# Stores and raw weight loads issued by GpSimd, and the reload of operands issued inside a group's last unit

## The chip, the cores and the metric

The kernel runs on one core of a Trainium2 chip. The metric is the device time of one execution in microseconds, as a median of several runs. A profiled execution has its own time, and its trace has a span, which is the time from the first to the last instruction.

## What is computed

An attention over channels feeds two multilayer perceptrons, for 6016 tokens, 256 channels and a hidden width of 2048:

```python
qn = q / (norm(q, axis=1) + 1e-06);  kn = k / (norm(k, axis=1) + 1e-06)
s = kn.transpose(0, 2, 1) @ qn / tau            # 256 x 256
a = exp(s - max); a /= a.sum(-1) + 1e-09
x = v @ a                                        # 6016 x 256
h = x @ w_in;   x = (h * sigmoid(1.702 * h)) @ w_out        # first perceptron
h = x @ w_in2;  out = where(h > 0, h, exp(min(h, 0)) - 1) @ w_out2   # second
```

## The kernel before

A first stage (to about 71 us) sums the squares of q and k and their product, makes the softmax, and folds it into the first weight matrix. After it there are two passes, A for the first perceptron and B for the second. The tokens are cut into six **groups** (b = 0 to 5) of 1024 tokens, the last of 896. A group is worked off in eight **units** (p = 0 to 7), each for 256 of the 2048 hidden columns. Pass A runs all its 48 units, then pass B its 48.

In a unit the first matrix product is made by seven products (`product`, i = 1 to 7, called in the order 1, 5, 6, 2, 7, 3, 4) of 2x2 blocks, whose operands are sums and differences of the blocks. Each operand and weight is held as a high and a low part, so a product is three matmuls (L637). Between them stand the 24 matmuls of the second matrix product of the unit before (L730 in pass A), so that a unit of pass A is 45 matmuls. ScalarE evaluates the activation (L667, L668) and copies two products between banks (L878 opens a unit, L885); VectorE adds (L889, L899) and makes low parts (L700).

The seven operands of a group (tiles `xA`, `xB`, one buffer for each i) are in SBUF while its eight units run. They are made well ahead, in the background of earlier units: `operands(kind, b)` casts each high part on ScalarE (L399), subtracts the low part on VectorE (L403) into a staging tile (`xt`; the tag "st" has four buffers and is shared with `w3t`), and stores it to DRAM (`xdA`, `xdB`; L405). `load_x` (L131) brings it back when the group's turn comes. The seven loads of a group are issued behind its predecessor's last unit; load i can only start when the last unit's product i has been made, since there is one buffer.

Pass A's background also prepares the second perceptron's weights: `fetch` loads raw 64-bit weights (L172 for w1 and w3, L177 for w2 and w4; three buffers `raw`, filled again as they are freed), `rounds` turns them into 32-bit floats, `combine_w3` makes the seven sums of w3 and stores them (`w3d`, L301), and `split_lo` stores w4 (`w4d`, L248, from one buffer `w4t`). One round of this work, called far, is put into the background queue in each odd unit of groups 1 to 5. A background generator is advanced eight times in a unit, first in, first out.

Each engine runs its instructions in program order (a manual schedule). All DMAs are issued by SyncE (SP). A DMA that waits for a semaphore holds back all DMAs behind it on that queue.

The lines that put far work and reloads into a unit:

```python
if b and p % 2:
    queue.append(some(1, far))
step(t)
if p == NP - 1:
    finish(*nxt[:2])
    for i in (1, 5, 6, 2, 7, 3, 4):
        load_x(nxt[0], nxt[1], XOP[i])
```

Of the kernel before, what the change touches and what calls it, by code (L numbers as in the profile page):

```python
# [9 lines left out]
F32 = mybir.dt.float32  # L10
# [12 lines left out]
def kernel(  # L23
# [40 lines left out]
    nc = tc.nc  # L64
# [6 lines left out]
    NP = KF // 2  # L71
# [29 lines left out]
    xd = {  # L101
        (kind, b): dr.tile([P, 7, 2, wid[b]], F32, name=f"xd{kind}{b}")
        for kind in "AB"
        for b in range(NG)
    }
    w3d = [dr.tile([P, 2, 2, 7, P], F32, name=f"w3d{i}") for i in range(NP // 2)]
    w4d = [dr.tile([P, 2, 2, C], F32, name=f"w4d{i}") for i in range(NP)]
# [3 lines left out]
    XOP = {1: 0, 2: 1, 3: 2, 4: 3, 5: 4, 6: 5, 7: 6}  # L111
# [13 lines left out]
    def x_tile(kind, b, i):  # L125
        x_t[kind, b, i] = xp.tile([P, 2, BANK], F32R, tag=f"x{i}", name=f"x{kind}")
        return x_t[kind, b, i]

    def load_x(kind, b, i):
        n = wid[b]  # L130
        nc.sync.dma_start(out=x_tile(kind, b, i)[:, :, :n].bitcast(F32), in_=xd[kind, b][:, i, :, :])  # L131
# [13 lines left out]
    order = [("w1", 0), ("w1", 1), ("w2", 0), ("w1", 2), ("w1", 3), ("w2", 1), ("w2", 2)]  # L145
    order += [("w1", 4), ("w1", 5), ("w2", 3), ("w2", 4), ("w1", 6), ("w1", 7)]
    order += [("w2", i) for i in range(5, NWP)]
    NEAR = len(order)
# [7 lines left out]
    w1s = {}  # L156
    state = {"done": -1, "auto": False, "freed": 0}

    def fetch(x=None):

        n = place[x] if x else next(ring, None)
        if n is None:
            return
        name, i = order[n]
        if x:
            t = wts.tile([P, WP, 2], I32, tag=f"wB{ASIDE[x]}", name="raw")
        else:
            t = cv.tile([P, WP, 2], I32, tag="raw", name="raw", bufs=RAWS)
        w = dram[name]
        if name in ("w1", "w3"):  # L170
            f, c = divmod(i, KC)
            nc.sync.dma_start(  # L172
                out=t.rearrange("p f t -> p (f t)"),
                in_=w[c * P:(c + 1) * P, f * WP:(f + 1) * WP].bitcast(I32),
            )
        else:
            nc.sync.dma_start(  # L177
                out=t.rearrange("p (f d) t -> p f (d t)", f=2),
                in_=w[i * 2 * P:(i + 1) * 2 * P, :].bitcast(I32).rearrange(
                    "(f p) d -> p f d", p=P  # L180
                ),
            )
        raws[n] = t
# [32 lines left out]
    ends = {}  # L216
# [16 lines left out]
    def shaped(n):  # L233
        t = live[n].bitcast(F32)
        return t if order[n][0] == "w1" else t.rearrange("p (f d) -> p f d", f=2)
# [6 lines left out]
    def split_lo(n):  # L242
        if order[n][0] == "w3":
            return
        hi, lo = target(n)
        nc.vector.tensor_sub(lo, shaped(n), hi.bitcast(F32))
        if order[n][0] == "w4":
            nc.sync.dma_start(out=w4d[order[n][1]], in_=ends.pop(n).bitcast(F32))  # L248

    def combine(f0, f1, part, done=None):  # L250

# [35 lines left out]
    def combine_w3(n):  # L287

        c = order[n][1] // KC
        ts = {}  # L290

        def part(x, i, m):
            g, i0, k = (0, 0, 3) if i < 3 else (1, 3, 4)
            if (x, g) not in ts:
                ts[x, g] = stage([P, 2, k, P], "w3t")
            return ts[x, g][:, :, i - i0:i - i0 + m, :]

        def store(g):
            r = slice(0, 3) if g == 0 else slice(3, 7)
            for x in range(2):  # L300
                nc.sync.dma_start(out=w3d[c][:, x, :, r, :], in_=ts[x, g].bitcast(F32))  # L301

        return combine(live[n - 1].bitcast(F32), live[n].bitcast(F32), part, store)

# [56 lines left out]
    made = set()  # L361
# [18 lines left out]
    def operands(kind, b, direct=False):  # L380

        n = wid[b]
        t = full.pop((kind, b))
        b11, b12 = (t[:, 0, i * n:(i + 1) * n] for i in range(2))
        b21, b22 = (t[:, 1, i * n:(i + 1) * n] for i in range(2))
        temp = {}

        def sub(i, x, y):
            temp[i] = stg.tile([P, BANK], F32, tag="t", name="tt", bufs=3)
            nc.vector.tensor_sub(temp[i][:, :n], x, y)  # L390

        def tgt(i):
            if direct:
                return x_tile(kind, b, i)
            return stage([P, 2, BANK], "xt")

        def hi(i, x):
            d = hold_t[i] = tgt(i)
            nc.scalar.copy(d[:, 0, :n], x)  # L399

        def lo(i, x):
            d = hold_t[i]
            nc.vector.tensor_sub(d[:, 1, :n], x, d[:, 0, :n].bitcast(F32))  # L403
            if not direct:
                nc.sync.dma_start(out=xd[kind, b][:, i, :, :], in_=d[:, :, :n].bitcast(F32))  # L405

        hold_t = {}
        hi(0, b11)
        sub(4, b12, b11)
        yield False  # L410
        hi(1, b21)
        lo(0, b11)
        yield False
        hi(2, b22)
        lo(1, b21)
        yield False
        hi(4, temp[4][:, :n])
        sub(5, b22, temp[4][:, :n])
        yield False
        lo(2, b22)  # L420
        lo(4, temp[4][:, :n])
        yield False
        hi(5, temp[5][:, :n])
        sub(6, b22, b12)
        yield False
        hi(6, temp[6][:, :n])
        lo(5, temp[5][:, :n])
        yield False
        sub(3, b21, temp[5][:, :n])
        lo(6, temp[6][:, :n])  # L430
        yield False
        hi(3, temp[3][:, :n])
        yield False
        lo(3, temp[3][:, :n])
        made.add((kind, b))
        yield False
# [40 lines left out]
    with tc.manual_schedule():  # L477
        make_identity(nc, ident)

        with ExitStack() as st:  # L480
# [24 lines left out]
            for i, m in enumerate(CHUNKS):  # L505
# [7 lines left out]
                if i == 4:  # L513
                    nc.sync.dma_start(
                        out=tau_sb,
                        in_=tau.rearrange("(o a) -> o a", o=1).to_broadcast([P, 1]),
# [20 lines left out]
                for s in range(m):  # L537
                    for c in range(KC):
# [4 lines left out]
                            start=(j0 + s == 0),  # L543
# [12 lines left out]
            for i in range(2):  # L556
                for c in range(KC):
                    x = i * KC + c
                    nc.tensor.matmul(
                        n_ps[:, x:x + 1], acc[:, i, c * P:(c + 1) * P], ones[:, 0:1],  # L560
                        start=True, stop=True,
# [12 lines left out]
            for c in range(KC):  # L574
                nc.tensor.matmul(
                    rq_ps[:, c * P:(c + 1) * P], rn[:, c:c + 1].to_broadcast([P, P]), ident,
                    start=True, stop=True,
# [13 lines left out]
            for c in range(KC):  # L591
                nc.vector.scalar_tensor_tensor(
                    out=e[:, c, :], in0=s_ps[c][:, :C], scalar=rk[:, c:c + 1], in1=rq,
# [34 lines left out]
        units = [(kind, b, p) for kind in "AB" for b in range(NG) for p in range(NP)]  # L628
        g_t = {}

        def product(dst, i, u, start):
            kind, b, p = u
            n = wid[b]
            w = w_first[kind, p // 2]
            x = x_t[kind, b, XOP[i]]
            for k, (wi, xi) in enumerate(((0, 0), (0, 1), (1, 0))):
                nc.tensor.matmul(  # L637
                    dst[:, :n],
                    w[:, wi, p % 2, WOP[i], :],
                    x[:, xi, :n],  # L640
                    start=(start and k == 0),
                    stop=(k == 2),
                    skip_group_check=True,
                )
# [334 lines left out]
        for b in range(NG):  # L979
# [6 lines left out]
            nxt = units[units.index(("A", b, 7)) + 2]  # L986
            plan_at(nxt, lambda b=b: queue.append(operands("B", b)))

        for t in range(len(units) + 1):
            u = units[t] if t < len(units) else None  # L990
            if u:
                kind, b, p = u
                if kind == "A" and b == 0 and p:
                    need("w2", min(p, NP - 1))
                if u == ("B", 0, 0):
                    passA.close()
                    tp = ctx.enter_context(tc.tile_pool(name="tpB", bufs=1))
                for f in plan.get(u, []):
                    f()
                if kind == "A":  # L1000
                    if b == 0:
                        queue.append(some(12, near) if p < 5 else some(12, last_near))
                    if b and p % 2:
                        queue.append(some(1, far))
            step(t)
            if u is None:
                break

            if p == NP - 1:
                nxt = units[t + 1] if t + 1 < len(units) else None  # L1010
                if nxt:
                    finish(*nxt[:2])
                    for i in (1, 5, 6, 2, 7, 3, 4):
                        load_x(nxt[0], nxt[1], XOP[i])
            if kind == "A" and b == NG - 1:
                if p % 2:
                    c = p // 2
                    nc.sync.dma_start(out=first_weights("B", c).bitcast(F32), in_=w3d[c])
                if p:
                    need("w4", p - 1)  # L1020
                    nc.sync.dma_start(out=second_weights("B", p - 1).bitcast(F32), in_=w4d[p - 1])
                if p == NP - 1:
                    need("w4", p)
            if u == ("B", 0, 0):
                nc.sync.dma_start(out=second_weights("B", NP - 1).bitcast(F32), in_=w4d[NP - 1])
# [29 lines left out]
```

## Time and profile before

| | |
|---|---|
| median of 3 runs | 1117.41 us (1115.81 to 1118.59) |
| profiled execution | 1117.26 us, of which the trace spans 1115.5 us |
| TensorE (PE) busy | 1071.8 us, 96% |
| VectorE (DVE) busy | 818.3 us, 73% |
| ScalarE (ACT) busy | 779.8 us, 70% |
| GpSimd (POOL) busy | 1.9 us, 9 instructions |
| DMA queue of SP | 143.41 MB, 35.3% of 16 engines' span |

PEld is the weight load of TensorE, SPq the DMA-issuing queue of SyncE. In rows, "L637" is line 637 of the kernel, `b<-xA,wAA` says that tiles xA and wAA are read and a PSUM bank b is written, and the bracket at the end says how long the engine had been idle and what ended it. Matmuls are pipelined, so neighbouring PE rows overlap a little.

### The profile page before, as it was taken

The numbers are of one execution on the slowest core, as the hardware profiler recorded it, in microseconds if no ns is written. First come the engines' busy times: TensorE is split into PE (matmuls) and PEld (weight loads), VectorE is DVE, ScalarE is ACT, GpSimd is POOL, SyncE is SP. The second block draws the span as 40 slices with busy tenths as digits, with TensorE's granted clock in tenths as the row PEclk, the third lists the DMA queues.
The fourth block names the chain that finished last, engine by engine and source line by source line (L and its number), as shares of the span: only waits on it lengthen the run. The fifth ranks groups of instructions, "written<-read, shape, count | busy, mean of one in ns | idle before, by whom it ended". The sixth has DMA issues, their size and how long they took to land.

```text
span 1115.5 us, 15490 instructions
## 1 busy us (share of the span) xinstructions
PE 1071.8 (96%) x5846; PEld 934.4 (84%) x5846; DVE 818.3 (73%) x1326; ACT 779.8 (70%) x1463; POOL 1.9 (0%) x9
## 2 busy tenths in 40 slices
PE   7979999998997998998999999999999999999998
PEld 6767878886886887887889899999899999899998
DVE  5888776564664773664634998888888888888886
ACT  5778777765775774875745867867767767777776
POOL 0000000000000000000000000000000000000000
PEclk9999999998998999999999999999999999999999
DMA  9912165236546564543558114003003103003100
GB/s 334 343 49 95 38 240 193 95 126 230 212 169 217 187 256 170 189 151 136 214 197 316 58 66 149 39 1 133 38 1 132 39 1 132 39 1 108 46 1 34
DMA packets 47355, 144.40 MB, mean 129 GB/s; under 512 B 4528, under 2 KB 14000, under 8 KB 46768
## 3 DMA queue, kind: packets, MB, share of 16 engines
q1 hardware_dynamic: 47280, 143.41, 35.3%
q8 instruction: 46, 0.75, 0.3%
q14 instruction: 29, 0.24, 0.1%
HBM read 86.25 MB, written 57.15 MB: 129 GB/s over the span
## 4 chain that ended last, share of the span: by engine, by line
PE 80%; DVE 7%; ACT 6%; DMA 5%; issue 1%; SPq 0%; ACTq 0%; DVEq 0%
PE b L637 36%; PE b L754 20%; PE b L730 20%; DMA qk<-in_k_dram 2%; DMA xA<-xdA 2%; DVE ee L684 1%; DVE gg L689 1%; DMA w4d<-w4t 1%; DVE g L700 1%; PE b L539 1%; ACT ee L673 1%; PE b L448 1%; ACT th L674 1%; PE b L370 1%; ACT g L696 1%
## 5 line engine op out<-in xcount | busy, mean ns | idle before, releaser
L754 PEld LDWEIGHTS b<-wBB,g 128*128 128x128 f32 x2256 | 301.6, 190 | 21.2 <-DVE g L700 2.3
L754 PE MATMUL b<-wBB,g 128*128 128x256 f32 x2256 | 308.9, 282 | 1.3 <-DVE g L700 1.0
L730 PE MATMUL b<-g,wBA 128*128 128x512 f32 (+1 forms) x1152 | 301.3, 390 | 1.7 <-DVE g L700 1.7
L637 PE MATMUL b<-xA,wAA 128*128 128x512 f32 (+1 forms) x1008 | 271.1, 393 | 25.4 <-DMA xA<-xdA 17.7
L637 PE MATMUL b<-xB,wAB 128*128 128x512 f32 (+1 forms) x1008 | 267.8, 389 | 0.2 <-DVE b L889 0.2
L730 PEld LDWEIGHTS b<-g,wBA 128*128 128x128 f32 x1152 | 218.6, 191 | 43.7 <-DVE g L700 2.2
L637 PEld LDWEIGHTS b<-xA,wAA 128*128 128x128 f32 x1008 | 189.8, 190 | 64.8 <-issue 19.3
L637 PEld LDWEIGHTS b<-xB,wAB 128*128 128x128 f32 x1008 | 174.1, 189 | 21.0 <-DVE b L889 0.4
L696 ACT CAST g<-gg 128x512 fp32r<-128x512 f32 (+1 forms) x192 | 118.4, 617 | 93.2 <-DVE gg L689 93.1
L889 DVE TENSOR_TENSOR b<-b,s 128x512 f32<-128x512 f32 (+1 forms) x96 | 66.0, 687 | 145.6 <-PE b L637 142.3
L684 DVE SCALAR_TENSOR_TENSOR ee<-ee,th 128x512 f32<-128x512 f32 (+1 forms) x192 | 129.8, 676 | 31.9 <-ACT th L674 31.7
L667 ACT ACTIVATE g<-b 128x512 fp32r<-128x512 f32 (+1 forms) x144 | 85.0, 591 | 84.2 <-PE b L637 83.8
L700 DVE TENSOR_TENSOR g<-gf,g 128x512 fp32r<-128x512 f32 (+1 forms) x192 | 128.6, 673 | 19.0 <-ACT gf L668 18.7
L700 DVE TENSOR_TENSOR g<-gg,g 128x512 fp32r<-128x512 f32 (+1 forms) x192 | 129.3, 674 | 11.0 <-ACT g L696 6.5
L673 ACT ACTIVATE ee<-b 128x512 f32<-128x512 f32 (+1 forms) x144 | 84.6, 587 | 34.7 <-PE b L637 34.5
L689 DVE SCALAR_TENSOR_TENSOR gg<-b,ee 128x512 f32<-128x512 f32 (+1 forms) x144 | 97.9, 680 | 4.9
L899 DVE TENSOR_TENSOR c<-b,s 128x512 f32<-128x512 f32 (+1 forms) x96 | 64.6, 673 | 41.6 <-PE b L637 41.4
L668 ACT ACTIVATE gf<-b 128x512 f32<-128x512 f32 (+1 forms) x144 | 84.5, 587 | 2.0 <-DVE g L700 1.6
L674 ACT ACTIVATE th<-b 128x512 f32<-128x512 f32 (+1 forms) x144 | 84.1, 584 | 0.0
L878 ACT COPY b<-b 128x512 f32<-128x512 f32 (+1 forms) x96 | 56.3, 587 | 34.3 <-PE b L637 34.2
L885 ACT COPY s<-b 128x512 f32<-128x512 f32 (+1 forms) x96 | 56.2, 586 | 32.4 <-PE b L637 31.9
L539 PE MATMUL b<-qk 128*128 128x256 f32 x188 | 44.5, 394 | 7.4 <-DMA qk<-in_k_dram 7.3
(91 smaller groups left out, 692.3 us busy)
## 6 DMA issues: line engine op xcount, KB each, us to landing
xdB<-xt SPq DMA_DIRECT2D x35, 512.0 KB, 2.9
xB<-xdB SPq DMA_DIRECT2D x35, 512.0 KB, 5.3
xdA<-xt SPq DMA_DIRECT2D x28, 512.0 KB, 2.9
xA<-xdA SPq DMA_DIRECT2D x28, 512.0 KB, 6.4
raw<-in_moe_w_in_dram SPq DMA_DIRECT2D x16, 512.0 KB, 6.1
raw<-in_moe_w_out_dram SPq DMA_DIRECT2D x16, 512.0 KB, 4.0
wAB<-w3d SPq DMA_DIRECT2D x4, 1792.0 KB, 8.5
v_raw<-in_v_dram SPq DMA_DIRECT2D x11, 512.0 KB, 4.5
```

Of the source, the lines that this page charges most:

```text
L637: nc.tensor.matmul(dst[:, :n], w[:, wi, p % 2, WOP[i], :], x[:, xi, :n], start=(start and k == 0), stop=(k == 2), skip_group_check=True,)
L667: nc.scalar.activation(self.sl(ik)[0], h, AF.Gelu_apprx_sigmoid)
L668: nc.scalar.activation(t[:, :n], h, AF.Gelu_apprx_sigmoid)
L673: nc.scalar.activation(e[:, :n], h, AF.Exp)
L674: nc.scalar.activation(t[:, :n], h, AF.Tanh, scale=0.5)
L684: nc.vector.scalar_tensor_tensor(out=e[:, :n], in0=e[:, :n], scalar=1.0, in1=t[:, :n], op0=ALU.add, op1=ALU.mult,)
L689: nc.vector.scalar_tensor_tensor(out=g[:, :n], in0=h, scalar=0.0, in1=e[:, :n], op0=ALU.max, op1=ALU.min)
L696: nc.scalar.copy(self.sl(ik)[0], self.tmp[ik][:, :self.n])
L700: nc.vector.tensor_sub(lo, self.tmp.pop(ik)[:, :self.n], hi.bitcast(F32))
L730: nc.tensor.matmul(bank[a][:, :n], w[:, f, wi, d * P:(d + 1) * P], g[:, gi, k * n:(k + 1) * n], start=fresh((kind, b, a)), stop=(p == NP - ...
L754: nc.tensor.matmul(bank[a][:, s % 2 * C:(s % 2 + 1) * C], g[:, gi, s * P:(s + 1) * P], w[:, f, wi, :], start=fresh((kind, b, a)), stop=(p ...
L889: nc.vector.tensor_add(bank[c][:, :n], bank[b][:, :n], s5[:, :n])
```

## The change

GpSimd now issues the stores of operands (`xdA`, `xdB`), of w3's sums and of w4, and the loads of raw weights of w3 and w4 (those from place NEAR on). SP keeps all other DMAs. The reload of operand i is issued behind product i of a group's last unit, if the next group's operands have been made. Far work is put into the queue in even units instead of odd ones.

```diff
+    def queue_of(n):
+        return nc.gpsimd if n >= NEAR else nc.sync
@@ fetch
-            nc.sync.dma_start(
+            queue_of(n).dma_start(
...
-            nc.sync.dma_start(
+            queue_of(n).dma_start(
@@ split_lo
-            nc.sync.dma_start(out=w4d[order[n][1]], in_=ends.pop(n).bitcast(F32))
+            nc.gpsimd.dma_start(out=w4d[order[n][1]], in_=ends.pop(n).bitcast(F32))
@@ combine_w3
-                nc.sync.dma_start(out=w3d[c][:, x, :, r, :], in_=ts[x, g].bitcast(F32))
+                nc.gpsimd.dma_start(out=w3d[c][:, x, :, r, :], in_=ts[x, g].bitcast(F32))
@@ operands
-                nc.sync.dma_start(out=xd[kind, b][:, i, :, :], in_=d[:, :, :n].bitcast(F32))
+                nc.gpsimd.dma_start(out=xd[kind, b][:, i, :, :], in_=d[:, :, :n].bitcast(F32))
@@
+        loaded = set()
+
+        def load_next(u, i):
+
+            if u[2] < NP - 1 or u not in units[:-1]:
+                return
+            nxt = units[units.index(u) + 1][:2]
+            if nxt in made and nxt + (i,) not in loaded:
+                loaded.add(nxt + (i,))
+                load_x(*nxt, XOP[i])
+
         def product(dst, i, u, start):
+            product_(dst, i, u, start)
+            load_next(u, i)
+
+        def product_(dst, i, u, start):
@@ the loop over units
-                    if b and p % 2:
+                    if b and p % 2 == 0:
                         queue.append(some(1, far))
...
-                        load_x(nxt[0], nxt[1], XOP[i])
+                        load_next(u, i)
```

On SP, ahead of the reload for group 2 of pass A (`xA<-xdA_86`), there stood before (`x7` is a run of seven):

```order
L131 DMA xA<-xdA_85 128x1024 x7
L405 DMA xdB_90<-xt 128x1024 x6
L358 DMA v_raw<-in_v_dram 128x1024
L405 DMA xdB_90<-xt 128x1024
L358 DMA v_raw<-in_v_dram 128x1024
L172 DMA raw<-in_moe_w_in_dram 128x1024
L405 DMA xdA_86<-xt 128x1024 x7
L172 DMA raw<-in_moe_w_in_dram 128x1024 x2
L301 DMA w3d_96<-w3t 128x2x384 x2
L131 DMA xA<-xdA_86 128x1024 x7
L301 DMA w3d_96<-w3t 128x2x512 x2
```

and now, on the same engine:

```order
L131 DMA xA<-xdA_85 128x1024 x7
L363 DMA v_raw<-in_v_dram 128x1024 x2
L131 DMA xA<-xdA_86 128x1024 x7
L363 DMA v_raw<-in_v_dram 128x1024 x2
L131 DMA xA<-xdA_87 128x1024 x7
```

The stores and raw loads are gone from between two reloads; the loads of v, which belong to units 2 and 3 of a group, are left.

What left SP stands on POOL in this order, from the first operands stored in pass A on:

```order
L410 DMA xdA_85<-xt 128x1024 x7
L410 DMA xdB_90<-xt 128x1024 x7
L177 DMA raw<-in_moe_w_in_dram 128x1024 x2
L410 DMA xdA_86<-xt 128x1024 x7
L177 DMA raw<-in_moe_w_in_dram 128x1024
L306 DMA w3d_96<-w3t 128x2x384 x2
L306 DMA w3d_96<-w3t 128x2x512 x2
L177 DMA raw<-in_moe_w_in_dram 128x1024
L410 DMA xdB_91<-xt 128x1024 x7
```

The order of the stores among themselves is the old one, and no reload stands among them.

On ACT, around the last unit of group 1 of pass A, there stood before (the first row opens the last unit; L197 and L198 scale raw weights, L259 casts sums of w3 into `w3t`):

```order
L878 COPY b2_78<-b3_79 128x512
L885 COPY s5_2012<-b0_76 128x512
L197 ACTIVATE raw_1712<-raw_1712 128x512
L198 ACTIVATE raw_1712<-raw_1712 128x512
L667 ACTIVATE g_2040<-b3_79 128x512
L668 ACTIVATE gf_2039<-b3_79 128x512
L667 ACTIVATE g_2040<-b1_77 128x512
L668 ACTIVATE gf_2062<-b1_77 128x512
L259 CAST w3t_2068<-bits_1629 128x2x128
L259 CAST w3t_2068<-bits_1719 128x2x256
```

and now, where the row of L898 is the copy that opens the last unit:

```order
L264 CAST w3t_1999<-bits_1438 128x2x128
L264 CAST w3t_1999<-bits_1650 128x2x256
L687 ACTIVATE g_2016<-c22_1944 128x512
L688 ACTIVATE gf_2015<-c22_1944 128x512
L264 CAST w3t_2020<-s_1997 128x2x256
L264 CAST w3t_2020<-s_1998 128x2x256
L687 ACTIVATE g_2016<-b1_77 128x512
L688 ACTIVATE gf_2034<-b1_77 128x512
L898 COPY b2_78<-b3_79 128x512
L905 COPY s5_2037<-b0_76 128x512
L687 ACTIVATE g_2073<-b3_79 128x512
```

The far work of a group's last unit has moved into the unit before it, and the last unit is left with none.

## Rows read from the trace of the kernel before

**Rows 1.** The page: busy time of TensorE.

```profile
PE 1071.8 (96%) x5846; PEld 934.4 (84%) x5846; DVE 818.3 (73%) x1326; ACT 779.8 (70%) x1463; POOL 1.9 (0%) x9
```

**Rows 2.** Waits of TensorE, 70 to 620 us: total us, times, longest us.

```profile
PE b L637 <- DMA xA<-xdA: 17.7, 4, 5.7
```

**Rows 3.** Windows: length, busy us of each engine (instructions), granted clock, DMA share, GB/s.

```profile
core 0: us, PE busy (x) PEld busy (x) DVE busy (x) ACT busy (x) POOL busy (x), PEclk, DMA share, GB/s
230.90:241.08 10.18, 10.18 (x46) 8.45 (x45) 4.29 (x7) 5.41 (x12) 0.00 (x0) 1.00 0.16 52
241.08:269.43 28.35, 22.86 (x91) 18.42 (x90) 12.95 (x23) 14.63 (x28) 0.00 (x0) 0.88 0.60 213
332.65:361.40 28.75, 23.01 (x91) 18.51 (x90) 12.95 (x23) 14.63 (x28) 0.00 (x0) 0.88 0.60 210
424.62:450.57 25.95, 22.29 (x91) 17.95 (x90) 10.07 (x16) 13.27 (x25) 0.00 (x0) 0.93 0.50 182
514.06:538.69 24.63, 21.78 (x91) 18.08 (x90) 9.73 (x16) 12.77 (x25) 0.00 (x0) 0.93 0.44 152
538.69:596.34 57.65, 55.47 (x271) 50.55 (x270) 30.13 (x51) 34.57 (x72) 0.00 (x0) 1.00 0.60 224
568.98:578.10 9.12, 9.12 (x46) 8.45 (x45) 3.56 (x6) 4.83 (x11) 0.00 (x0) 1.00 0.57 238
269.43:332.65 63.22, 63.22 (x287) 52.09 (x286) 44.49 (x75) 47.69 (x90) 0.00 (x0) 1.00 0.51 188
```

**Rows 4.** Timeline at the end of group 1, PE and SPq: start, us, engine, line.

```profile
240.20 0.84 PE L637 MATMUL b<-xA,wAA 128*128 128x512 f32 x3
...
249.12 2.43 SPq L301 DMA_DIRECT2D w3d<-w3t  x2
...
251.65 3.76 SPq L131 DMA_DIRECT2D xA<-xdA  x7
...
256.05 1.62 PE L637 MATMUL b<-xA,wAA 128*128 128x512 f32 x3 [5.49 <-DMA xA<-xdA]
```

**Rows 5.** Windows: the four microseconds behind that wait.

```profile
256.00:260.00 4.00, 3.95 (x9) 3.14 (x10) 0.00 (x0) 0.57 (x1) 0.00 (x0) 0.50 1.03 420
```

**Rows 6.** The reload in pass B: SP's waits, and landing at one boundary (676 to 700 us).

```profile
SPq L131 <- PE b L637: 292.6, 48, 61.4
...
xB<-xdB SPq DMA_DIRECT2D x7, 512.0 KB, 4.5
```

**Rows 7.** The page, DMA issues: count, KB each, median us from issue to landing.

```profile
xdB<-xt SPq DMA_DIRECT2D x35, 512.0 KB, 2.9
...
xA<-xdA SPq DMA_DIRECT2D x28, 512.0 KB, 6.4
...
w3d<-w3t SPq DMA_DIRECT2D x8, 512.0 KB, 3.8
```

**Rows 8.** Timeline of two staged sets of operands: pass B's first, then pass A's.

```profile
276.90 0.62 ACT L399 CAST xt<-tt 128x512 fp32r<-128x512 f32 x1 [0.26 <-DMA xdB<-xt]
...
280.33 0.60 ACT L878 COPY b<-b 128x512 f32<-128x512 f32 x1
...
281.47 1.52 PE L637 MATMUL b<-xA,wAA 128*128 128x512 f32 x6
...
309.98 3.33 SPq L405 DMA_DIRECT2D xdA<-xt  x4
...
314.10 0.62 ACT L399 CAST xt<-tt 128x512 fp32r<-128x512 f32 x1
```

**Rows 9.** Timeline of the set stored in group 0, ACT and PEld.

```profile
152.82 0.63 ACT L399 CAST xt<-tt 128x512 fp32r<-128x512 f32 x1 [1.42 <-DMA xdA<-xt]
...
159.16 0.99 PEld L637 LDWEIGHTS b<-xA,wAA 128*128 128x128 f32 x5 [2.01 <-ACT b L878]
```

**Rows 10.** Timeline of a w4 store in group 5, SPq and ACT.

```profile
555.93 0.32 SPq L248 DMA_DIRECT2D w4d<-w4t  x1
...
564.31 0.62 ACT L240 CAST w4t<-bits 128x512 fp32r<-128x512 f32 x1 [5.26 <-DMA w4d<-w4t]
```

**Rows 11.** GpSimd's longest instruction (groups by line), and two of VectorE (timeline).

```profile
L567 POOL TENSOR_TENSOR rn<-rn,half 128x4 f32<-128x4 f32 x1 | 1.0, 1028 | 56.6 <-ACT warm L566 56.6
...
286.88 0.69 DVE L208 SCALAR_TENSOR_TENSOR bits<-raw,bits 128x512 int32<-128x512 int32 x1
287.48 0.42 DVE L202 TENSOR_SCALAR bits<-raw 128x512 int32<-128x512 int32 x1
```

## The prediction

> **What bounds the kernel now.** I read the busy times first: TensorE is busy for 96% of the span [rows 1], so a gain can only be time in which it stands still or runs slowly. Next come its waits. In pass A the longest in total is for the reload of the operands, four waits of 17.7 us together [rows 2]. The windows then say where TensorE loses time. A clean unit of pass A takes 10.18 us, with TensorE busy throughout, and six units with all their background work and v's transposes take 63.22 us, busy for all 63.22 [rows 3]: away from the group boundaries ScalarE and VectorE keep up. At a boundary that is not so. The timeline of the end of group 1 shows why: the last unit's product 1 starts at 240.20 us, so its operand's buffer is free at about 241; the reload is issued at 251.65, behind two stores of w3's sums at 249.12 that had to wait for their data, and TensorE starts again at 256.05 after 5.49 us of idling [rows 4]. In the four microseconds after that the granted clock is 0.50, the lower of the two levels, 1.2 GHz [rows 5], so the wait costs more than its length. Pass B has the same reload, but there SP waits for TensorE (292.6 us in all), which is to say that the load stands ready at the queue's head when the buffer comes free [rows 6], and TensorE hardly waits.
>
> **What is lost, from windows.** I take the last unit of a group and the first of the next as one pair. A clean pair is 2 x 10.18 = 20.36 us. The pairs at the ends of groups 1, 2 and 3 take 28.35, 28.75 and 25.95 us [rows 3]: 7.99 + 8.39 + 5.59 = 21.97 us too long. At the end of group 4 the second unit belongs to the short group, whose clean unit is 9.12 us [rows 3]; its 21 first-product matmuls are short and its 24 second-product matmuls still belong to group 4, so it should take 21/45 x 9.12 + 24/45 x 10.18 = 9.69 us, and the pair 19.87; it takes 24.63, 4.76 too long. Six units of group 5 take 57.65 where 6 x 9.12 = 54.72 would do, 2.93 too long [rows 3]; in them ScalarE waits 5.26 us for the buffer of w4, whose store SP issued only at 555.93, behind weight loads that had become due [rows 10]. Together 21.97 + 4.76 + 2.93 = 29.66 us.
>
> **The change, part by part.** *Stores and raw loads leave SP.* SP then holds nothing between two reloads but loads of v from units 2 and 3. So load i is issued when product i of the last unit is done, a whole unit of 10.18 us before that product's next turn. Landing took 6.4 us at the median in pass A and 4.5 at a boundary of pass B [rows 7, 6], where seven loads also come within one unit. I therefore take all four boundaries as repaired, and the w4 store of group 5 as well, which no longer stands behind weight loads. Gain 29.66 us. *The reload inside the last unit* changes nothing by itself: the order of SP's rows would be the same if it were issued behind the unit, since nothing stands between. I cost it at nothing, for this reason. *Far work in even units* takes the raw scaling and the casts of w3 out of the last unit. The cover for it is the slack of ScalarE in the other units (47.69 busy of 63.22 us [rows 3]); cost nothing. If the first unit of a group could not hide it, some tenths per boundary would come back.
>
> *What GpSimd's issue costs.* GpSimd is otherwise idle after the first stage (1.9 us busy [rows 1]), so its own time is free. What counts is how much later a store lands, L, since a staging buffer is freed by that. The queue's order is that of the data, so nothing is held behind another's data, and only these waits can grow:
> - Pass B's operands, staged in unit 1 of groups 1 to 5, five sets. The fifth cast waits already, 0.26 us, for the first store [rows 8]. ScalarE then runs without a gap up to the next unit's copy, which ends at 280.33 + 0.60 = 280.93, while the matmuls that need it start at 281.47 [rows 8]: 0.54 us of slack. Cost 5 x (L - 0.54).
> - Pass A's operands, staged in units 4 and 5, four sets. First store at 309.98, landed 2.9 later [rows 7], fifth cast at 314.10 [rows 8]: slack 1.2 us. Cost 4 x (L - 1.2).
> - The set of group 0. A cast waits 1.42 us, and TensorE then waits 2.01 us for the late copy [rows 9], so there is no slack: cost L.
>
> No row has a DMA issued by GpSimd. The bounds: at best L = 0, the same landing as now. At worst the landing of 6.4 us that a reload has among six others, L = 3.5. A price by nearness: a 512 KB store in twice as many pieces (w3's sums) lands after 3.8 instead of 2.9 us, 0.9 later, and GpSimd's one small software operation takes 1.03 us [rows 7, 11]. I take L = 0.9: 5 x 0.36 + 0 + 0.9 = 2.7 us. With L = 2 it is 7.3 + 3.2 + 2 = 12.5 us; with L = 3.5, 14.8 + 9.2 + 3.5 = 27.5.
>
> The Trainium skill (DMA: Bandwidth & Descriptors, section on the anatomy of one DMA on the gpsimd path) gives such a DMA a fixed 2.0 us plus its bytes over 436 GB/s, which for 512 KB is an estimate of 3.2 us, 0.3 more than the row's 2.9. By that rule the cost would be 0.3 us instead of 2.7, and the time 1087.9 us; no run here shows it yet.
>
> **The sum.** The profiled execution took 1117.26 us (its span is 1115.5); the median of the runs shown is 0.15 above it, so I make no correction. 1117.26 - 29.66 + 2.7 = 1090.3 us, a gain of 27 us or 2.4%. For judging, 0.3% (3.4 us) is about what a measurement of this kernel can tell from no change.
>
> **The rivals.**
> - *Stores wait for VectorE.* If preparing a DMA on GpSimd has to wait out an instruction of VectorE, each store lands 0.69 us later still [rows 11], as VectorE is busy 44.49 of 63.22 us [rows 3]. L = 1.6: 5 x 1.06 + 4 x 0.4 + 1.6 = 8.5 us, 1096 us. For it: stores come just behind VectorE's own subtractions. Against: nothing in this trace shows GpSimd waiting for VectorE. The Trainium skill (SBUF - State Buffer, the summary of rules for kernel authors) speaks against issuing a DMA from GpSimd beneath VectorE work: descriptors are starved while VectorE runs in its faster modes. Here an instruction of that kind would be the raw shift, 0.42 us for 512 columns against 0.69 for one with two inputs [rows 11], and it is rare.
> - *The reload is still late.* In the last unit seven loads of 512 KB need most of what the DMA engines moved at their fullest (420 GB/s [rows 5]; 3.67 MB in 10.18 us is 360), and w3's stores of the unit before reach into it. If half of the loss at the four boundaries stayed (13.4 us): 1104 us. Against: pass B does the same without a wait.
> - *Slower.* GpSimd's issue is so slow that staging buffers run out. The cost is 10 L - 7.5 (the three terms added), so it eats the gain at L = 3.7, and from L = 4.1 (a store landing after 7 us) the kernel is slower by over 0.3%. At L = 5 it is 42.5 us, 1130 us. The place is ScalarE's cast in units 1 and 4, the wait that shows is the one of 0.26 us grown. For it: loads among six others take 6.4 us to land; seven stores come within some ten microseconds, each needing GpSimd. Against: at 1.03 us for a software operation GpSimd keeps up with one store in 1.4 us.
> - *It doesn't do what it says:* the reloads stay where they were in time, and 1117 us stays. Against: SP's new order has nothing in front of them.
>
> **How the numbers follow.** Forecast (all boundaries repaired, L from 0 to 2, so 1087.6 to 1100; most likely 1090): 0.71. Stores wait for VectorE: 0.13. Reload still late: 0.06. No effect: 0.04. Slower: 0.06. The first three are faster by over 0.3%: 0.90; same 0.04; slower 0.06. The range starts at 1086, the end with L = 0 less half the spread of the three runs, and goes to 1104 to take in the first two rivals; no effect and slower, 1 in 10, are left out.
>
> **What would show it.** Right: reloads in pass A issued from the copy that opens the last unit on, no wait of TensorE for `xA`, granted clock 1.00 at the boundaries, pairs of about 20.4 us, and the wait for w4's buffer gone. The stores' landing on GpSimd gives L directly, and waits of ScalarE's casts for `xdB` of up to about 1 us in five places give its cost. Wrong: TensorE waiting for `xA` in spite of early issue (reload still late), or ScalarE's casts waiting several microseconds and the bank copy late behind them (slower). Were stores to land after 7 us or more, the sign would be wrong; were the time below 1086, group 0, which I left untouched, would have gained too.

## The result, and the profile after

The changed kernel takes 1092.61 us (median of 4 runs, 1089.24 to 1094.07) beside 1116.61 for the kernel before: a ratio of 0.978, 95% interval 0.9761 to 0.9799. The profiled execution took 1094.07 us. The forecast was 1090.3, with a range of 1086 to 1104.

From the page of the changed kernel: busy times, the two DMA queues (q1 is SP's, q0 GpSimd's) and three DMA issues.

```profile
PE 1066.0 (98%) x5846; PEld 931.2 (85%) x5846; DVE 819.8 (75%) x1326; ACT 778.9 (71%) x1463; POOL 72.0 (7%) x126
...
q1 hardware_dynamic: 25568, 84.03, 21.4%
q0 software_dynamic: 16144, 59.38, 14.6%
...
xdB<-xt POOLq DMA_DIRECT2D x35, 512.0 KB, 3.5
...
xdA<-xt POOLq DMA_DIRECT2D x28, 512.0 KB, 3.5
xA<-xdA SPq DMA_DIRECT2D x28, 512.0 KB, 6.4
```

Stores issued by GpSimd land 3.5 us after their issue, where they took 2.9 [rows 7]; the reload's median is the old one. Next, SP's timeline at the end of group 1, and TensorE's waits between 70 and 620 us:

```profile
240.98 8.48 SPq L131 DMA_DIRECT2D xA<-xdA  x7
```

```profile
PE b L657 <- ACT b L898: 5.3, 4, 2.2
PE b L657 <- DVE c L919: 2.8, 1, 2.8
PE b L750 <- DVE g L720: 1.7, 1, 1.7
```

The seven loads now go out one by one over 8.48 us, from the last unit's first product on, where they went out together over 10 us later [rows 4]. No wait for `xA` is left of the 17.7 us [rows 2]. The windows of the four pairs at the boundaries (last unit of a group and first of the next), then of six units of group 5, and of all of group 5:

```profile
core 0: us, PE busy (x) PEld busy (x) DVE busy (x) ACT busy (x) POOL busy (x), PEclk, DMA share, GB/s
241.74:261.38 19.64, 19.64 (x88) 16.28 (x87) 10.51 (x17) 12.83 (x25) 2.13 (x4) 1.00 0.86 315
325.39:345.34 19.95, 19.95 (x88) 16.12 (x87) 10.65 (x17) 12.83 (x26) 2.44 (x4) 1.00 0.87 310
408.63:429.03 20.40, 20.40 (x91) 16.89 (x90) 10.26 (x16) 13.21 (x25) 1.29 (x2) 1.00 0.70 257
492.09:512.01 19.92, 19.92 (x92) 16.90 (x90) 9.37 (x15) 11.71 (x24) 0.55 (x1) 1.00 0.56 188
512.01:573.16 61.15, 57.96 (x271) 52.83 (x270) 28.53 (x48) 33.97 (x71) 4.27 (x8) 0.94 0.54 202
...
502.22:582.37 80.15, 76.96 (x362) 69.74 (x361) 37.50 (x63) 45.14 (x94) 4.82 (x9) 0.96 0.55 205
```

The pairs took 28.35, 28.75, 25.95 and 24.63 us [rows 3]; TensorE is now busy throughout them at a granted clock of 1.00. Two pairs fall below 20.36 because the copy that opens the last unit, from which I count, comes late there. Group 5 has become worse: its six units took 57.65 us [rows 3] and now take 61.15. Its timeline shows a new stall (SP's, GpSimd's and ScalarE's rows; then the landing of the store of 519.83, and windows):

```profile
516.56 0.53 POOL L410 DMA_DIRECT2D xdB<-xt  x1 [7.07 <-DVE xt L408]
517.55 0.53 POOL L410 DMA_DIRECT2D xdB<-xt  x1 [0.46 <-DVE xt L408]
519.30 0.33 SPq L1038 DMA_DIRECT2D wAB<-w3d  x1
519.83 1.13 POOL L410 DMA_DIRECT2D xdB<-xt  x2 [1.74 <-DVE xt L408]
...
529.30 0.62 ACT L404 CAST xt<-tt 128x512 fp32r<-128x512 f32 x1 [5.63 <-DMA xdB<-xt]
```

```profile
DMA to landing us min/median/max: 9.4/9.4/9.4
```

```profile
528.00:532.00 4.00, 1.16 (x4) 0.74 (x4) 1.89 (x4) 2.70 (x6) 0.53 (x1) 0.79 1.03 420
532.00:536.00 4.00, 4.00 (x12) 3.52 (x12) 1.72 (x4) 2.09 (x5) 0.53 (x1) 0.50 0.80 316
```

The load of pass B's first weights, 1.8 MB, goes out at 519.30, half a microsecond ahead of the third store of operands. That store lands after 9.4 us; the seventh cast needs its buffer and holds ScalarE for 5.63 us; TensorE runs out of work, and then works at a granted clock of 0.50, the 1.2 GHz level. Before, six stores stood in front of this load on SP.

From ScalarE's opening copies, the whole profiled gain up to pass B (605.54 - 582.37 = 23.17 us; pass B is as long as it was) comes out by group: groups 1 to 4 gain 6.41 + 8.19 + 5.52 + 4.98 = 25.10 us, and what lies before group 1 gains 0.11. Group 5 loses 2.04: its first unit, the second half of the last pair, gains 1.47 (11.26 to 9.79 us), and the rest loses 3.51.

### The profile page after: what moved, and what is told of

Read it like the earlier page. It is cut to its first block, busy times and chain, and to the rows that moved or that the text cites. A ratio compares the mean times of both kernels' runs of the same rounds, so it can differ in the third digit from the quotient of the medians.

```text
span 1092.3 us, 15514 instructions
## 1 busy us (share of the span) xinstructions
PE 1066.0 (98%) x5846; PEld 931.2 (85%) x5846; DVE 819.8 (75%) x1326; ACT 778.9 (71%) x1463; POOL 72.0 (7%) x126
## 4 chain that ended last, share of the span: by engine, by line
PE 57%; issue 22%; DVE 6%; ACT 6%; POOL 4%; DMA 4%; SPq 0%; POOLq 0%; ACTq 0%
PE b L657 26%; PE b L774 20%; PE b L750 8%; DMA qk<-in_k_dram 2%; DVE ee L704 1%; DVE gg L709 1%; POOL xdB L410 1%; POOL xdA L410 1%; ACT ee L693 1%; PE b L544 1%; PE b L453 1%; ACT th L694 1%; POOL w3d L306 1%; DMA xdB<-xt 1%; DVE g L720 1%
## 5 line engine op out<-in xcount | busy, mean ns | idle before, releaser
L657 PE MATMUL b<-xA,wAA 128*128 128x512 f32 (+1 forms) x1008 | 267.9, 389 | 9.1 <-ACT b L898 5.3
L898 ACT COPY b<-b 128x512 f32<-128x512 f32 (+1 forms) x96 | 56.2, 585 | 19.0 <-PE b L657 18.9
```

What stands on the lines that cost most here:

```text
L657: nc.tensor.matmul(dst[:, :n], w[:, wi, p % 2, WOP[i], :], x[:, xi, :n], start=(start and k == 0), stop=(k == 2), skip_group_check=True,)
```

## The experiments

All ratios are to the kernel before, with their 95% intervals. **Theory 1**: the reload was held only by DMAs in front of it on SP, so each of the change's three parts frees it alone. **Rival A**: the issue inside the unit does it. **Rival B**: GpSimd's queue does it. Two more are on the new stall of group 5. **Theory 2**: the first weight load, no longer held on SP, passes the stores of operands, and a store behind it lands late. **Rival C**: the stores land late because GpSimd issues them.

### One part at a time

*Queue only* (far work in odd units, reload behind the unit):

```diff
-                    if b and p % 2 == 0:
+                    if b and p % 2:
...
             product_(dst, i, u, start)
-            load_next(u, i)
```

> Edit: only the stores and raw loads go to GpSimd; far work stays in odd units and the reload stays behind the last unit. Theory 1 (the reload was only held back by other DMAs in front of it on SP, so any one of the three parts frees it): SP has nothing in front of the reload, all four pairs of pass A are clean (19.6 to 20.4 us), TensorE waits 0 us for xA; group 5 keeps the stall of ScalarE's cast that the changed kernel shows (5 to 6 us); about 1092 us, ratio 0.978 as the whole change. Rival A (issuing the reload inside the last unit is what repairs the boundaries): no gain at the boundaries, 1113 to 1117 us. Rival B (GpSimd's queue is what repairs them): as theory 1, 1092 us.

Measured: 1094.51 us, ratio 0.980 (0.9781 to 0.982), no wait for `xA`, pairs of 19.92 to 20.56 us, and the cast of group 5 waits 5.7 us. A wait for w4's buffer of 2.96 us is left in group 5.

*Far work in even units only* (the kernel before with one condition changed):

```diff
-                    if b and p % 2:
+                    if b and p % 2 == 0:
```

> Edit: only the far work goes to even units; all DMAs stay on SP, the reload stays behind the last unit. Theory 1: the stores of the last unit's far work are gone from in front of the reload, which is issued some 5 us after the last unit opens and lands in 4 to 5 us, so TensorE waits under 1 us for xA in each of four places; group 5 has neither the wait for w4 nor for xdB, since weight loads stand behind the stores on SP; 1087 to 1091 us, at or below the whole change. Rivals A and B: the boundaries stay as they were (22 to 27 us lost), 1112 to 1117 us.

Measured: 1089.27 us, ratio 0.9755 (0.9738 to 0.9772). SP's timeline at the end of group 1, and TensorE's wait:

```profile
240.24 7.23 SPq L301 DMA_DIRECT2D w3d<-w3t  x4
247.56 4.13 SPq L131 DMA_DIRECT2D xA<-xdA  x7
```

```profile
PE b L637 <- DMA xA<-xdA: 0.9, 2, 0.5
```

The four stores of w3 still stand in front of the reload, but have their data a unit earlier. The reload comes just in time.

*Reload inside the last unit only* (the change with far work in odd units and every DMA on SP; the stores of w3 and w4 as the one shown):

```diff
     def queue_of(n):
-        return nc.gpsimd if n >= NEAR else nc.sync
+        return nc.sync
...
-                nc.gpsimd.dma_start(out=xd[kind, b][:, i, :, :], in_=d[:, :, :n].bitcast(F32))
+                nc.sync.dma_start(out=xd[kind, b][:, i, :, :], in_=d[:, :, :n].bitcast(F32))
...
-                    if b and p % 2 == 0:
+                    if b and p % 2:
```

> Edit: only the reload is issued inside the last unit; all DMAs stay on SP, far work stays in odd units. Theory 1: four loads are issued before the unit's raw load and three behind it, all before the stores of w3, so the four pairs are clean; the wait for w4 in group 5 (2.9 us) is left; about 1090 us. Rival A: the same, about 1090 us. Rival B: the boundaries stay, 1112 to 1117 us.

Measured: 1089.56 us, ratio 0.9754 (0.974 to 0.9769). SP's timeline:

```profile
240.21 3.72 SPq L131 DMA_DIRECT2D xA<-xdA  x4
245.69 0.33 SPq L177 DMA_DIRECT2D raw<-in_moe_w_in_dram  x1
246.12 2.56 SPq L131 DMA_DIRECT2D xA<-xdA  x3
248.78 6.71 SPq L306 DMA_DIRECT2D w3d<-w3t  x4
```

Four loads stand in front of the raw load and three behind it, all ahead of w3's stores; TensorE waits for `xA` once, for 0.5 us. The wait for w4's buffer in group 5 stays (4.2 us). So each part alone brings nearly the whole gain: theory 1 holds, and rivals A and B, which each want one part, fall.

*The change with the reload behind the unit:*

```diff
             product_(dst, i, u, start)
-            load_next(u, i)
```

> Edit: the whole change, but the reload is issued behind the last unit as before. Theory 1 (SP has nothing in front of the reload, so where the program issues it changes nothing): 1091 to 1094 us, as the whole change; reloads start at the last unit's first product. Rival A (the issue inside the unit does something of its own): 1096 us or more, with waits of TensorE for xA.

Measured: 1094.01 us, ratio 0.9803 (0.9787 to 0.9819), against 0.978 (0.9761 to 0.9799): the same within the intervals, and SP's seven loads take 8.48 us again, from 241.94. Once SP is free, where the program issues the reload changes nothing that can be measured.

### What GpSimd's queue costs

*The change with every DMA of GpSimd back on SP* (the stores of w3 and w4 as the one shown):

```diff
-        return nc.gpsimd if n >= NEAR else nc.sync
+        return nc.sync
...
-                nc.gpsimd.dma_start(out=xd[kind, b][:, i, :, :], in_=d[:, :, :n].bitcast(F32))
+                nc.sync.dma_start(out=xd[kind, b][:, i, :, :], in_=d[:, :, :n].bitcast(F32))
```

> Edit: the whole change, but every DMA that GpSimd issues goes back to SP. Theory 1 and rival A: boundaries clean, and as weight loads of group 5 stand behind the stores of operands on SP again, neither of the two stalls of group 5 shows; staged casts wait 0.25 us instead of 0.8; about 1087 us, 4 to 7 us below the whole change. Rival B: the gain is gone, 1112 to 1117 us.

Measured: 1086.84 us, ratio 0.9736 (0.9719 to 0.9753), the lowest median of the study, and with its interval below that of the whole change (0.9761 to 0.9799). SP's rows in group 5, and the group's window:

```profile
514.06 7.12 SPq L410 DMA_DIRECT2D xdB<-xt  x6
521.28 0.41 SPq L1038 DMA_DIRECT2D wAB<-w3d  x1
```

```profile
499.99:573.85 73.86, 73.86 (x361) 67.53 (x360) 37.40 (x63) 45.12 (x94) 0.00 (x0) 1.00 0.61 223
```

Six stores stand in front of the weight load again, and group 5 is busy throughout.

*The change with the first weight load later*, so that it can't meet the stores:

```diff
-                if p % 2:
+                if p in (3, 5, 7):
                     c = p // 2
...
+                if p == 2:
+                    nc.sync.dma_start(out=first_weights("B", 0).bitcast(F32), in_=w3d[0])
```

(the added lines stand behind the load of w4's part p - 1)

> Edit: the whole change, but the first weight load of 1.8 MB for pass B is issued in unit 3 of group 5, behind the load of w4's second part, instead of in unit 1. Theory 2 (in group 5 the weight load now overtakes the stores of operands, which land some 9 us late, so ScalarE's seventh cast waits 5.6 us): the cast waits under 1 us, group 5 takes about 74 us instead of 80; about 1087 us, as with no DMA on GpSimd. Rival C (the stores land late because GpSimd issues them): the wait of 4 to 6 us stays, 1092 us.

Measured: 1088.62 us, ratio 0.9758 (0.9741 to 0.9774); casts wait at most 0.85 us for `xdB`, and group 5 takes 74.10 us:

```profile
502.48:576.58 74.10, 73.98 (x361) 67.55 (x360) 37.40 (x63) 45.05 (x94) 4.83 (x9) 1.00 0.60 221
```

With all stores still on GpSimd, the stall is gone: it is the weight load that makes it, and rival C falls. The interval lies below that of the change with the reload behind the unit (0.9787 to 0.9819), which has the stall; with that of the change itself (0.9761 to 0.9799) it overlaps a little.

*Only the stores of operands back on SP:*

```diff
-                nc.gpsimd.dma_start(out=xd[kind, b][:, i, :, :], in_=d[:, :, :n].bitcast(F32))
+                nc.sync.dma_start(out=xd[kind, b][:, i, :, :], in_=d[:, :, :n].bitcast(F32))
```

> Edit: the whole change, but the stores of operands go back to SP; w3, w4 and raw loads stay on GpSimd. Theory 2: six of the seven stores stand in front of the weight load on SP again, the wait of 5.6 us in group 5 is gone and the casts wait 0.25 us; about 1087 us. Rival C: the same, about 1087 us. A theory by which any DMA on GpSimd costs time by itself: 1090 us or more.

Measured: 1088.5 us, ratio 0.9753 (0.9737 to 0.977); casts wait 0.2 us for `xdB`, group 5 takes 73.86 us. The other stores and the raw loads cost nothing that can be measured by being on GpSimd.

*Stores on SP, weight loads on GpSimd* (the version without GpSimd's DMAs, with one edit):

```diff
-                    nc.sync.dma_start(out=first_weights("B", c).bitcast(F32), in_=w3d[c])
+                    nc.gpsimd.dma_start(out=first_weights("B", c).bitcast(F32), in_=w3d[c])
```

> Edit: no store and no raw load on GpSimd (all on SP, as in the version without GpSimd), but the four weight loads of 1.8 MB on GpSimd, so that they pass the stores. Theory 2: the seventh cast of group 5 waits 4 to 6 us again although SP issues the stores, group 5 takes 78 to 80 us; 1091 to 1093 us. Rival C: no wait, 1087 us as without GpSimd.

Measured: 1087.45 us, ratio 0.9749 (0.9733 to 0.9765), no long wait. The time came out as rival C had it, and my number was wrong; the landings tell the two apart. GpSimd issues the load at 520.87, and SP the third store at 520.9 too. The landing of the stores issued at 520.9 and 521.5, and of the next two:

```profile
DMA to landing us min/median/max: 2.7/6.1/9.5
```

```profile
DMA to landing us min/median/max: 8.8/8.9/8.9
```

The third store lands after 2.7 us, and it alone frees the buffer that the seventh cast needs. The three behind it land after 8.8 to 9.5 us, nearly as late as GpSimd's behind the weight load (9.4 to 10.5), although SP issued them. So the lateness is that of a store behind a big load, from either queue, and rival C falls here too. In the changed kernel the load was half a microsecond ahead of the third store and here it was level with it: whether ScalarE stalls hangs on that.

*Late stores:* to the version with the weight load later, work on GpSimd is added ahead of each store of operands.

```diff
             if not direct:
+                nc.gpsimd.tensor_copy(pause[:, :1], d[:, 1, :1].bitcast(F32))
+                for _ in range(3):
+                    nc.gpsimd.memset(pause, 0.0)
                 nc.gpsimd.dma_start(out=xd[kind, b][:, i, :, :], in_=d[:, :, :n].bitcast(F32))
```

> Edit: the kernel with the first weight load in unit 3, and ahead of each store of operands GpSimd reads one column of the staged tile and fills a small tile three times, some 1.1 us, so that each of these stores lands that much later. The prediction's formula for L, the extra landing (5 x (L - 0.54) + 4 x (L - 1.2) + L): L goes from 0.6 to about 1.7, the cost from 0.9 to 9.5 us, so about 8.6 us more, 1097 us, with the fifth cast of each set waiting about 1.9 us. Rival D (ScalarE and VectorE make up for late casts in the slack of pass A, the slack of 0.54 us is not one): 0 to 3 us more, 1088 to 1091 us.

Measured: 1118.09 us, ratio 1.0011 (0.9995 to 1.0027): the whole gain is gone, 29 us where I had expected 8.6. GpSimd's rows in unit 1 of group 2 (the first two stores), then VectorE's that end the staged tiles, then ScalarE and TensorE:

```profile
277.48 0.18 POOL L411 COPY pause<-xt 128x1 f32<-128x1 f32 x1 [8.75 <-DVE xt L409]
277.72 1.05 POOL L413 MEMSET pause<- 128x256 f32 x3
278.96 0.55 POOL L414 DMA_DIRECT2D xdB<-xt  x1 [0.19 <-issue]
279.51 0.72 POOL L411 COPY pause<-xt 128x1 f32<-128x1 f32 x1
280.28 1.05 POOL L413 MEMSET pause<- 128x256 f32 x3
281.81 0.53 POOL L414 DMA_DIRECT2D xdB<-xt  x1 [0.47 <-DVE xt L409]
```

```profile
276.66 0.68 DVE L409 TENSOR_TENSOR xt<-vt,xt 128x512 fp32r<-128x512 f32 x1
277.69 0.69 DVE L409 TENSOR_TENSOR xt<-vt,xt 128x512 fp32r<-128x512 f32 x1 [0.34 <-ACT xt L405]
```

```profile
281.97 0.62 ACT L405 CAST xt<-tt 128x512 fp32r<-128x512 f32 x1 [2.10 <-DMA xdB<-xt]
...
286.33 0.60 ACT L902 COPY b<-b 128x512 f32<-128x512 f32 x1
...
286.98 1.66 PE L661 MATMUL b<-xA,wAA 128*128 128x512 f32 x6 [2.11 <-ACT b L902]
```

The first store is issued 1.6 us after its data (277.34 to 278.96), and the fifth cast waits 2.10 us, both near what I had expected. The second is issued 3.4 us after its data (278.38 to 281.81), since each store now holds GpSimd for 2 us and more and the next waits behind it; the sixth cast waits too (1.19 us). So L of a set, which I had put at 1.7, was about 3. For L = 3.2, near the second store's delay, the formula gives 10 x 3.2 - 7.5 = 24.5 us, 23.6 more than at 0.6. In this set the next copy comes 13.66 us after the last (272.67 to 286.33), where it was 11.08 in the changed kernel (261.38 to 272.46): 2.6 us more, as 3.2 - 0.54 says.

By group the formula fits less well. Beside the version with the weight load later, groups 1 to 4 grew by 15.30 us together, where it gives 18.4; group 0 grew by 6.41 and group 5 by 7.88, where it gives 2.6 each. In these two TensorE waited 5.43 and 4.42 us for a late copy, and in the unit behind it the mean granted clock was 0.72 and 0.71, which the formula has no term for. That the sum comes near the 29 us is in part luck. Rival D, that ScalarE catches up, falls.

## Why the prediction was right, and where it was off

- *The boundaries.* Right in mechanism and size. Of the 26.73 us that I took from the four pairs, groups 1 to 4 and the first unit of group 5 gained 25.10 + 1.47 = 26.57. The reload was late only because it stood behind other DMAs on SP; three different edits that put it in front of them, or those away, each bring 1089 to 1095 us.
- *The reload inside the last unit changes nothing by itself.* True beside the other two parts (0.9803 against 0.978). Alone, with the stores left on SP, it is worth the whole gain, since it then changes SP's order. The far work in even units, which I gave no gain, is worth as much alone (0.9755). The forecast credits the queue with all four boundaries, where any one of the three parts would have done.
- *Group 5, the wait for w4.* Its 2.93 us went, but not for the reason that I gave. I had read that SP issued the store late, behind weight loads. VectorE's part of the data was done at 555.22 + 0.69 = 555.91 us, and SP issued the store at 555.93 [rows 10]; late was its landing. From the kernel before, VectorE's row and the landing of that store:

```profile
555.22 0.69 DVE L246 TENSOR_TENSOR w4t<-bits,w4t 128x512 fp32r<-128x512 f32 x1
```

```profile
DMA to landing us min/median/max: 8.4/8.4/8.4
```

With only the queue changed 2.96 us of the wait stay. With only the far work moved the store still lands after 9.9 us, on SP, but no later cast of the pass needs its buffer, and the wait is gone. So it was the far work that removed it.
- *Group 5, the new stall.* Instead of gaining, the group became 2.04 us longer. The step that failed is the sentence that, since the queue's order is that of the data, "nothing is held behind another's data, and only these waits can grow". It looked at what is left behind each DMA on its old queue, and not at what a DMA had held back there: with the stores gone from SP, the weight load of 1.8 MB passed them. The trace before had the sign: the one store of operands that SP issued behind this load, at 552.31, landed 10.7 us later, and no cast waited for it. Without that stall the group takes 73.86 to 74.10 us, so it cost 6 us in the profiled execution. Part of this is chance: in the profiled execution of the change with the reload behind the unit the cast waits as long (5.55 us), but the granted clock does not fall, and the group takes 77.34 us:

```profile
503.38:580.72 77.34, 74.24 (x361) 67.46 (x360) 37.49 (x63) 45.03 (x94) 4.81 (x9) 1.00 0.58 213
```

So some 3 us of the 6 are the stall and the other 3 the clock behind it; why it fell in one execution and not in the other is open.
- *L.* I took 0.9, and it is 0.6 (3.5 against 2.9). The fifth cast waits 0.81 to 0.85 us instead of 0.21 to 0.26 in groups 1 to 4, and TensorE does not notice, as a slack of 0.54 us had it. Of 2.7 us for GpSimd some 0.5 came, in group 0, where the unit with the late cast grew from 12.41 to 12.86 us. The rule of the Trainium skill (DMA: Bandwidth & Descriptors, on the anatomy of a DMA on the gpsimd path) gives an estimate of 3.2 us for 512 KB, 0.3 below the 3.5 measured; my 0.9 on top of the row's 2.9 was 0.3 above it.
- *The sum.* The miss of 4 us is the difference of two larger ones. The six units of group 5 took 61.15 us where I had 54.72, 6.43 more, and GpSimd's price came to 0.5 us instead of 2.7. That the time came this near is in part luck.
- *The rivals.* Stores that wait for VectorE: not seen, L is below what I had without them. The slower case: with late stores the gain was just eaten at an L of about 3, where I had 3.7; the formula holds roughly, and not group by group.

What stays open: the first stage and group 0 differ by 2 us and more between profiled executions of versions that are alike there (group 0 takes 96.47 to 98.54), so that the 1 to 2 us between the version without GpSimd's DMAs and those that only lack the stall are not explained. In the profiled executions that difference lies ahead of group 1, and their intervals overlap.

## What to carry to other kernels

Look at a DMA queue as a list of waits: here a load whose buffer was free was late because of what stood in front of it, and moving either of the two mended it. A reorder on the same queue did so without the new stall. When DMAs leave a queue, ask not only what was waiting behind them, but also what they had been holding back: a big load set free may pass the small stores on whose landing an engine's buffers hang. Look in the trace before for a small DMA that already goes out behind the big one; here two did, and landed after 8.4 and 10.7 us. And ask how much later a store may land before the unit behind it grows: in this kernel it was half a microsecond.

## What the runs showed that was not expected

A DMA issued by GpSimd keeps that engine busy for 0.53 to 0.74 us. Stores of operands land 3.5 us after their issue there, against 2.9 on SP [rows 7]; but with work on GpSimd ahead of each of them they too land after 2.9, and why is not shown. The 512 KB stores of w3's sums, in smaller pieces, land after 6.0 us at the median in the changed kernel, against 3.8 before [rows 7]. That isn't GpSimd's doing, since they take 6.3 in the version without its DMAs. In both they go out beside the reload; with only the far work moved, where they stand ahead of it, they take 4.1. A store of operands (512 KB) issued just behind the load of 1.8 MB landed after 8.8 to 11.2 us, from either queue, three to four times its usual time, though the two move in opposite directions between SBUF and memory.
